# Attention with a gated unit on one core: store buffers moved, three weight scalings on VectorE, and the exponential table loaded later

## The chip, the cores and the metric

The kernel runs on one core of one Trainium2 chip. The metric is the device time of the whole kernel in microseconds; a number of runs is given by its median. One more execution is taken with the hardware profiler, and all lines of profiles below come from such executions. PE is TensorE, PEld its weight loads, DVE is VectorE, ACT is ScalarE, POOL is GpSimd, SP is SyncE.

## The reference

Input `x` has 2048 rows of 640. It is normalised, and two things are computed from it: an attention over the last 512 keys and values of a cache with 32 heads of 192, and a gated unit with 1536 inner columns. All inputs are bfloat16.

```
W = min(4096, max(256, Sk // 4))                  # 512 of 2048 keys
q = (x @ wq).reshape(B, Sq, 32, 192)              # wq: 640 x 6144
k, v = k_cache[:, :, Sk-W:, :], v_cache[:, :, Sk-W:, :]
p = softmax(q k^T * 192 ** -0.5)
s = (p v).reshape(B, Sq, 6144) @ wo               # wo: 6144 x 640

h = sigmoid(x @ w_gate) * (x @ w_up)
g = silu(h @ w_down)
out = x0 + s * g          # x = layernorm(x0) in the formulas above
```

## The kernel before

**Two phases.** The first phase (to about 165 us) normalises `x`, transposes it, and computes the gated unit in four stages of 512 rows (`s` from 0 to 3). A stage ends with four parts `q`; each part multiplies by `w_down` (L495), takes a sigmoid on ACT (L502), a product on VectorE into a buffer `gB_sb` of `gpool` (L503), and stores it to DRAM from POOL's queue (L519). The second phase is the attention. It goes through 16 runs `r`, one for each pair of a group of four heads (`g`, 8 groups) and a half of the rows (`pi`).

**Order.** Every engine has its own instruction stream in the order in which the code emits it; nothing is reordered between engines, and waits are by semaphores. The pools of the two phases use the same memory: when the pools under `bctx` are closed, those of the second phase (`acc_pool` first, then `wo_pool`, `qT_pool`, `e_pool` for the exponentials, and so on) are laid from the same place, and an instruction that first writes a tile waits for the last users of what lay there before.

**Query projection by sums.** The queries are not one plain product with `wq`. Each weight chunk `c` (five of them, 128 of the 640 rows) comes as a tile `raw` (L202, from POOL's queue; three buffers), is multiplied by a power of two and turned to float16 in place (`scale_raw`, L216), and is then copied and combined into four weight tiles (`copy_w`, `sum_w`: L225 and L234 to L238 where POOL does it). `second_w(c)` (L240) does that for the second group on POOL, and then issues the load of the chunk three further on. The second group's weight tiles lie in the accumulator tile `acc_hi`, which is not needed until later. `query_slots` (L568) gives eleven slots of ten matmuls (L560). After a slot, partial sums go from PSUM to a ring of four buffers `qp` (L579 on ACT in the first run, L581 on VectorE in others), and sums of PSUM and such a partial make `qT` (L594, VectorE).

**Around the change.** In the last stage of the first phase the second group's chunks 0, 1 and 2 are scaled on ACT after parts 1, 2 and 3 (L510). Then the weights of the output projection are loaded (`load_wo(0)`, SP's queue), ACT computes one exponential of a dummy value so that its table of exponentials is loaded (L744), and the eleven slots of the first run follow; after the first three of them stand `second_w(0)`, `(1)` and `(2)`. Then run 0 begins: 16 score steps `k` (`stage_s`, L638: six matmuls L646 into one of two pairs of banks, then an exponential L650 on ACT), between which the slots for the next run's queries lie (`q_after`). After steps 7 and 11 of run 0 chunks 3 and 4 are scaled on ACT, each followed by its `second_w`. Then eight value stages (`stage_pv`, L652: 16 matmuls L660, a reciprocal L666 and a product L667 on VectorE into `o_st`); after each second one `o_st`, which has two buffers, is transposed by SP's queue (L673). The output projection (L703) of a run lies in the value part of the next one.

`scale_k` (L142) multiplies a key tile of the same shape as `raw` on VectorE.

Of the kernel before, what the change touches and what calls it, by code (L numbers as in the profile page):

```python
# [8 lines left out]
AF = mybir.ActivationFunctionType  # L9
ALU = mybir.AluOpType  # L10
BF16 = mybir.dt.bfloat16
F32 = mybir.dt.float32
F16 = mybir.dt.float16
# [4 lines left out]
def kernel(  # L18
# [13 lines left out]
    nc = tc.nc  # L32
# [46 lines left out]
    def bank2():  # L79
        if bank_order:  # L80
            b = bank_order.pop(0)
        else:
            b = ring.pop(0)
            ring.append(b)
        return ps_all[:, 2 * b:2 * b + 2, :]

    def flat(ps):
        return ps.rearrange("p b n -> p (b n)")
# [26 lines left out]
    mx, w_up, w_down = (w_sc[:, i:i + 1] for i in range(3))  # L115
# [61 lines left out]
    def scan_fold(wm, i):  # L177

        v = scan_t[i]
        bits = (wm[:] if i == 0 else v).bitcast(I32)  # L180
        nc.vector.tensor_single_scalar(bits, v.bitcast(I32), 0x7FFF7FFF, op=ALU.bitwise_and)
        if i > 0:
            nc.vector.tensor_tensor(wm[:], wm[:], v, ALU.max)
# [15 lines left out]
    def load_raw(g, c, eng):  # L199
        raw = raw_pool.tile([P, 2, GC], BF16, name="raw")  # L200
        for r in (LO, HI):
            eng.dma_start(raw[r], wq_r[:, c, :, g * GC:(g + 1) * GC])  # L202
        raw_t[g, c] = raw
# [9 lines left out]
    def sums_w(g, c, r, i):  # L213
        return w_t[g][i][r, c].rearrange("p (j h e) -> p h j e", h=2, e=HF)

    def scale_raw(g, c):  # L216
        raw = raw_t[g, c][:]
        nc.scalar.activation(raw.bitcast(F16), raw, AF.Copy, scale=w_up)  # L218

    def copy_act(dst, src):  # L220
        nc.scalar.activation(dst, src, AF.Copy)  # L221
# [1 line left out]
    def copy_w(g, c, copy):  # L223
        for k, r in enumerate((LO, HI)):
            copy(sums_w(g, c, r, 0), part_w(g, c, r, k, 0))  # L225

    def scale_w(g, c):
        scale_raw(g, c)
        copy_w(g, c, copy_act)

    def sum_w(g, c, tt=nc.vector.tensor_tensor, copy=copy_act):
        a = slice(0, P)
        TA, TB, TC = (sums_w(g, c, a, i) for i in range(1, 4))
        tt(TB, part_w(g, c, a, 1, 1), part_w(g, c, a, 0, 1), ALU.subtract)  # L234
        tt(TA, TB, part_w(g, c, a, 0, 0), ALU.add)
        copy(sums_w(g, c, HI, 2), part_w(g, c, HI, 1, 1))
        tt(TC, part_w(g, c, a, 1, 0), TA, ALU.subtract)
        tt(sums_w(g, c, HI, 1), part_w(g, c, HI, 0, 1), part_w(g, c, HI, 0, 0), ALU.subtract)  # L238

    def second_w(c):  # L240

        copy_w(1, c, nc.gpsimd.tensor_copy)
        sum_w(1, c, nc.gpsimd.tensor_tensor, nc.gpsimd.tensor_copy)
        load_raw(1 + (c + 3) // NCD, (c + 3) % NCD, nc.gpsimd)


    with ExitStack() as bctx:
        gpool = bctx.enter_context(tc.tile_pool(name="gpool", bufs=4))
        wB = bctx.enter_context(tc.tile_pool(name="wB", bufs=1))
        bwork = bctx.enter_context(tc.tile_pool(name="bwork", bufs=2))  # L250
        bone = bctx.enter_context(tc.tile_pool(name="bone", bufs=1))
        hpool = bctx.enter_context(tc.tile_pool(name="hpool", bufs=2))
        xpool = bctx.enter_context(tc.tile_pool(name="xpool", bufs=3))
        xin_pool = bctx.enter_context(tc.tile_pool(name="xin_pool", bufs=1))
        xt_pool = bctx.enter_context(tc.tile_pool(name="xt_pool", bufs=1))
# [177 lines left out]
        for s in range(NST):  # L433
# [57 lines left out]
            for q in range(TQ):  # L491
                oB_ps = flat(bank2())
                for f in range(NF):
                    for d0, dsz in d_chunks:
                        nc.tensor.matmul(  # L495
                            oB_ps[:, d0:d0 + dsz], lhsT=hT_sb[:, f, q * P:(q + 1) * P],
                            rhs=wd_sb[:, f, d0:d0 + dsz],
                            start=(f == 0), stop=(f == NF - 1),
                        )
                gB_sb = gpool.tile([P, D], BF16, name="gB_sb")  # L500
                sg = bone.tile([P, D], F32, name="sg")
                nc.scalar.activation(sg[:], oB_ps[:, 0:D], AF.Sigmoid)  # L502
                nc.vector.tensor_tensor(gB_sb[:], oB_ps[:, 0:D], sg[:], ALU.mult)  # L503
                if (s, q) in folds_q:
                    scan_fold(wmax, folds_q[s, q])
                if s == 3:
                    if q == 0:
                        scale_w(0, NCD - 1)
                    else:
                        scale_raw(1, q - 1)  # L510
                    if q == 1:
                        sum_w(0, NCD - 1)
                        load_raw(1, 2, nc.gpsimd)
                    if q < 3:
                        sum_x(pi, 3 + q, sw)
                    else:
                        load_k((1, 0))
                t = s * TQ + q
                nc.gpsimd.dma_start(gB_d[t * P:(t + 1) * P, :], gB_sb[:])  # L519
# [27 lines left out]
    def load_wo(g):  # L547
        pool = late["wo"] if g == NG - 1 else wo_pool
        eng = nc.scalar if 0 < g < NG - 1 else nc.sync
        wo_g = pool.tile([P, G * PC, D], BF16, name="wo_g")  # L550
        eng.dma_start(wo_g[:], wo_r[:, g * G * PC:(g + 1) * G * PC, :])
        wo_t[g] = wo_g
# [188 lines left out]
    last = len(runs) - 1  # L741
    qT_t, E_t, oT_t, ost_t = {}, {}, {}, {}
    load_wo(0)
    nc.scalar.activation(mx, w_up, AF.Exp, scale=0.0)  # L744
    slots = query_slots(0, True, (2, 3), (4, 5), (0, 1, 6))
    for n, k in enumerate((0, 1, 7, 2, 3, 8, 4, 5, 9, 6, 10)):
        slots[k]()
        if n < 3:
            second_w(n)
    sum_at = {0: (0,), 1: (1,), 3: (2,), 4: (3,), 6: (4,)}  # L750
    scale_at = {0: (2,), 3: (3,), 4: (4,)}
    q_after = {1: (0,), 2: (1,), 3: (2,), 4: (3,), 5: (4,), 6: (5, 6), 8: (7,), 10: (8,), 12: (9,), 14: (10,)}
# [1 line left out]
    for r, (pi, g) in enumerate(runs):  # L754
        s_list = [(i, pp, c) for i in range(2) for pp in range(G) for c in range(KC)]
        q_list = query_slots(r + 1, False, (0, 1), (2, 3), (2, 3, 1)) if r < last else []
        wo_list = [(r - 1, i, q) for i in range(2) for q in range(TQ)] if r > 0 else []
        for k, x in enumerate(s_list):
            stage_s(r, *x, k)
            for j in q_after.get(k, ()) if q_list else ():  # L760
                q_list[j]()
            if r == 0 and k in (7, 11):
                scale_raw(1, 3 + k // 8)
                second_w(3 + k // 8)
            if r == last and k % 2 == 1:
                ring[:] = [k // 2 % 2]
                stage_wo(*wo_list[k // 2])
        if r == last:
            wo_list = []
            bank_order[:] = [2, 3, 0, 1] * 2  # L770
        else:
            bank_order[:] = [0, 1, 0, 1] + [2, 3, 0, 1] * 3 if r > 0 else [2, 3, 0, 1] * 2
        ring[:] = [0, 1, 2, 3]

        new_t = g + 1 if pi == 0 and 0 < g < NG - 1 else None
        if new_t is not None:
            weight_tiles(new_t)
            scale_w(new_t, 0)
            scale_w(new_t, 1)
        elif pi == 1 and g + 1 < NG:  # L780
            scale_k((g + 1, 0))
            turn_k((g + 1, 0))
            load_k((g + 1, 1))
        if r == last - 1:
            qctx.close()
            for name, n in (("wo", 1), ("gate", 4 * TQ), ("fin", 2 * TQ), ("fout", 4), ("ost", 4), ("tmp", 2)):
                late[name] = ctx.enter_context(tc.tile_pool(name=f"late_{name}", bufs=n, **rs))
            load_wo(g)
            prepare(r)

        pv_list = [(i, pp, h) for i in range(2) for pp in range(G) for h in range(2)]
        done = 0
        for k, x in enumerate(pv_list):
            stage_pv(r, *x)
            if k == 3 and pi == 1 and g + 1 < NG:
                scale_k((g + 1, 1))
                turn_k((g + 1, 1))
                if g + 2 < NG:
                    load_k((g + 2, 0))
            share = (k + 1) * len(wo_list) // len(pv_list)  # L800
            while done < share:
                stage_wo(*wo_list[done])
                done += 1
            if new_t is not None:
                for c in sum_at.get(k, ()):
                    sum_w(new_t, c)
                    if c + 3 < NCD:
                        load_raw(new_t, c + 3, nc.gpsimd)
                for c in scale_at.get(k, ()):
                    scale_w(new_t, c)  # L810
        if new_t is not None and g + 2 < NG:
            for c in range(3):
                load_raw(g + 2, c, nc.gpsimd)
        if pi == 1 and g + 1 < NG:
            for pp in range(G):
                load_v(g + 1, pp, nc.scalar)
        if pi == 0 and 0 < g < NG - 1:
            load_wo(g)
        if r == last - 1:
            prepare(last)  # L820
# [32 lines left out]
```

The softmax here doesn't subtract the row's maximum and nothing guards it: scores larger than these inputs give would overflow.

## Time and profile before

| | |
|---|---|
| three timed runs, median | 914.24 us (913.92 to 914.3) |
| the profiled execution's own time | 915.81 us |
| its span in the trace | 914.0 us |
| granted clock of PE, mean over the span | 0.997 |
| PE busy | 894.2 us, 98% |
| VectorE busy | 650.2 us, 71% |
| ScalarE busy | 438.0 us, 48% |
| GpSimd busy | 178.6 us, 20% |
| DMA | 100.38 MB, mean 110 GB/s |

The profiled execution lasts 1.8 us longer than its span, which goes from the first to the last instruction in the trace. A line of a timeline gives start, duration, engine, line of the code, operation, output and inputs, how many were merged, and in brackets the idle time before it and what ended it. A line of the stretches gives, for each engine in the order PE, PEld, DVE, ACT, POOL, its busy time and how many instructions, then the clock granted to PE, the busy share of the DMA engines and GB/s.

### The profile page before, as it was taken

The page shows a single profiled execution, that of the slowest core. Times are in us where ns is not written, and L with a number is a line of the kernel's source. Part 1 is how long each engine was busy: PE and PEld are TensorE (multiplying, and loading weights), DVE is VectorE, ACT ScalarE, POOL GpSimd, SP SyncE. Part 2 cuts the span into 40 slices and gives each one's busy share as a digit, 9 for nine tenths or more (in the row PEclk, how much of TensorE's full clock was granted, in tenths as well). Part 3 has the DMA queues.
Part 4 walks back from the last instruction along what each step waited for, and adds up shares of the span by engine and source line. Part 5 has one row for each costly group of instructions (what it writes and reads, how often), then busy time and mean ns, then how long its engine had stood idle before and what let it go on. Part 6 is the DMA issues. An engine that isn't in the chain of part 4 may idle for free. (4 is left out here: it accounts for less than half of the span.)

```text
span 914.0 us, 18466 instructions
## 1 busy us (share of the span) xinstructions
PE 894.2 (98%) x7712; PEld 531.7 (58%) x7791; DVE 650.2 (71%) x1087; ACT 438.0 (48%) x513; POOL 178.6 (20%) x220
## 2 busy tenths in 40 slices
PE   8999999889999999999999999999999999999997
PEld 5545454446665656565656565656565656565665
DVE  4879956556667866786678667866786678666566
ACT  4323346673428542854285428542854285424240
POOL 0051112582000200020002000200020000001972
PEclk9999999999999999999999999999999999999999
DMA  9993374415271828193718271827192805264745
GB/s 287 259 267 91 93 153 94 117 53 89 41 133 10 190 45 131 20 172 53 131 19 182 41 134 18 182 45 130 18 180 43 134 17 132 42 116 138 158 112 122
DMA packets 186757, 100.38 MB, mean 110 GB/s; under 512 B 153584, under 2 KB 179056, under 8 KB 186672
## 3 DMA queue, kind: packets, MB, share of 16 engines
q1 hardware_dynamic: 157776, 57.85, 32.0%
q0 software_dynamic: 9408, 29.93, 14.3%
q10 hardware_dynamic: 19488, 11.41, 5.2%
q8 instruction: 61, 1.00, 0.5%
q14 instruction: 24, 0.20, 0.1%
HBM read 57.87 MB, written 5.24 MB: 69 GB/s over the span
## 5 line engine op out<-in xcount | busy, mean ns | idle before, releaser
L650 ACT ACTIVATE E<-ps_all 128x1024 bf16<-128x1024 f32 x256 | 253.4, 1022 | 308.2 <-PE ps_all L646 260.9
L703 PE MATMUL ps_all<-wo_g,oT 128*128 128x128 bf16 (+2 forms) x1480 | 225.2, 295 | 3.3
L646 PE MATMUL ps_all<-qT,kT 64*128 64x512 bf16 x1536 | 195.4, 376 | 4.1 <-ACT E L650 2.2
L660 PE MATMUL ps_all<-v_sb,E 128*128 128x193 bf16 x2048 | 189.5, 247 | 0.0
L660 PEld LDWEIGHTS <-E 128*128 128x128 bf16 x2048 | 168.6, 98 | 18.0 <-issue 6.4
L703 PEld LDWEIGHTS <-oT 128*128 128x128 bf16 x1542 | 121.4, 98 | 79.6 <-issue 3.6
L594 DVE TENSOR_TENSOR qT<-ps_all,qp 128x512 bf16<-128x512 f32 x176 | 116.8, 688 | 55.0 <-PE ps_all L560 45.0
L581 DVE COPY qp<-ps_all 128x512 f32<-128x512 f32 x150 | 100.8, 689 | 61.4 <-PE ps_all L560 61.4
L646 PEld LDWEIGHTS <-kT 64*128 64x128 bf16 x1536 | 75.8, 94 | 93.4 <-issue 10.7
L667 DVE TENSOR_TENSOR o_st<-ps_all,rden 128x768 bf16<-128x768 f32 x128 | 122.5, 957 | 9.6 <-DMA oT<-o_st 5.2
L202 POOL DMA_DIRECT2D raw<-in_A_wq_dram x80 | 48.0, 605 | 275.5 <-ACT wB L221 238.1
L135 POOL DMA_DIRECT2D k_sb<-in_A_k_cache_dram x32 | 32.7, 1027 | 277.1 <-DVE o_st L667 121.3
L218 ACT ACTIVATE raw<-raw,w_sc 128x1536 f16<-128x1536 bf16 x40 | 63.0, 1574 | 2.0 <-DMA raw<-in_A_wq_dram 1.1
L560 PE MATMUL ps_all<-XA,wA 64*128 64x512 f16 x420 | 54.0, 386 | 2.1 <-ACT qp L579 1.7
L560 PE MATMUL ps_all<-XB,wB 64*128 64x512 f16 x420 | 52.6, 376 | 0.4 <-ACT qp L579 0.4
L495 PE MATMUL ps_all<-wd_sb,hT_sb 128*128 128x128 bf16 (+1 forms) x377 | 52.4, 298 | 0.4
L560 PE MATMUL ps_all<-X,w 64*128 64x512 bf16 x420 | 51.9, 376 | 0.1
L738 DVE TENSOR_TENSOR acc<-ps_all,acc 128x640 f32<-128x640 f32 x48 | 39.5, 823 | 15.3 <-PE ps_all L703 14.9
L451 DVE TENSOR_TENSOR hT_sb<-ps_all,sig_sb 128x512 bf16<-128x512 f32 x48 | 32.4, 682 | 22.5 <-ACT sig_sb L450 11.8
L450 ACT ACTIVATE sig_sb<-ps_all 128x512 bf16<-128x512 f32 x48 | 28.0, 596 | 40.1 <-PE ps_all L445 37.1
L666 DVE RECIPROCAL rden<-ps_all 128x4 f32<-128x4 f32 x128 | 23.1, 181 | 33.0 <-PE ps_all L660 31.9
L738 DVE TENSOR_TENSOR acc_hi<-ps_all,acc_hi 128x640 f32<-128x640 f32 x48 | 39.3, 819 | 7.7 <-PE ps_all L703 7.7
(114 smaller groups left out, 744.3 us busy)
## 6 DMA issues: line engine op xcount, KB each, us to landing
raw<-in_A_wq_dram POOLq DMA_DIRECT2D x80, 192.0 KB, 3.8
k_sb<-in_A_k_cache_dram POOLq DMA_DIRECT2D x32, 192.0 KB, 6.0
wo_g<-in_A_wo_dram ACTq DMA_DIRECT2D x6, 960.0 KB, 6.9
v_sb<-in_A_v_cache_dram ACTq DMA_DIRECT2D x28, 192.0 KB, 3.9
gB_d<-gB_sb POOLq DMA_DIRECT2D x16, 160.0 KB, 3.7
gBa_sb<-gB_d SPq DMA_DIRECT2D x16, 160.0 KB, 4.1
xa_sb<-in_A_x_dram SPq DMA_DIRECT2D x16, 160.0 KB, 4.1
out_dram<-o_sb SPq DMA_DIRECT2D x15, 160.0 KB, 1.8
```

Of the source, the lines that this page charges most:

```text
L202: eng.dma_start(raw[r], wq_r[:, c, :, g * GC:(g + 1) * GC])
L218: nc.scalar.activation(raw.bitcast(F16), raw, AF.Copy, scale=w_up)
L495: nc.tensor.matmul(oB_ps[:, d0:d0 + dsz], lhsT=hT_sb[:, f, q * P:(q + 1) * P], rhs=wd_sb[:, f, d0:d0 + dsz], start=(f == 0), stop=(f == NF ...
L560: nc.tensor.matmul(ps_all[:, b, :], lhsT=w(r, c), rhs=x[r, c, :], start=(first and k == 0), stop=(k == len(cs) - 1), skip_group_check=True,)
L581: nc.vector.tensor_copy(dst, part(b))
L594: nc.vector.tensor_tensor(q_out(i, u, pp), part(b), t[:], ALU.add)
L646: nc.tensor.matmul(ps[:, b, :], lhsT=kT[h, c * PC + j, :], rhs=qT_t[r][i, j][h, pp, :], start=(j == 0), stop=(j == PC - 1),)
L650: nc.scalar.activation(E_t[r, i, pp][:, c, :, :], ps, AF.Exp, scale=scale_qk)
L660: nc.tensor.matmul(o_ps[:, q // 2, q % 2, 0:DH + 1], lhsT=E[:, c, h, q * P:(q + 1) * P], rhs=vt[:, c, 0:DH + 1], start=(c == 0), stop=(c = ...
L667: nc.vector.tensor_tensor(o_st[:, :, h * DH:(h + 1) * DH].rearrange("p (b i) d -> p b i d", b=2), o_ps[:, :, :, 0:DH], rden[:].to_broadcas ...
L703: nc.tensor.matmul(oA[:, d0 - base:d0 - base + dsz], lhsT=oT_t[r, i, pp][:, q * PC + j, :], rhs=wo_t[runs[r][1]][:, cc, d0:d0 + dsz], star ...
L738: nc.vector.tensor_tensor(acc[t][:], oA[:, 0:D], acc[t][:], ALU.add)
```

## The change

- The pool `gpool` of the gate's store buffers is opened after `hpool` instead of first. All of the first phase's pools that stood behind it move down, and its own place is now where the second phase has the tiles of exponentials `E`. The accumulators lie over weight tiles of the gated unit instead of over store buffers too.
- `scale_raw` can run on VectorE (a multiplication by the same scalar). Chunk 2 of the second group is scaled there after the seventh slot of the first run (n = 6, before its `second_w(2)`) instead of on ACT ahead of the slots, and `second_w(2)` itself moves from n = 2 to n = 6. Chunks 3 and 4 are scaled on VectorE after score steps 3 and 7 of run 0 instead of on ACT after steps 7 and 11, each again followed by its `second_w`.
- The dummy exponential with its table load comes after the third slot (n = 2) instead of ahead of the first.

The instructions of PE, POOL and SP are the same ones in the same order on each of these engines.

```diff
-    def scale_raw(g, c):
+    def scale_raw(g, c, on_act=True):
         raw = raw_t[g, c][:]
-        nc.scalar.activation(raw.bitcast(F16), raw, AF.Copy, scale=w_up)
+        if on_act:
+            nc.scalar.activation(raw.bitcast(F16), raw, AF.Copy, scale=w_up)
+        else:
+            nc.vector.tensor_scalar(raw.bitcast(F16), raw, w_up, None, op0=ALU.mult)
...
-        gpool = bctx.enter_context(tc.tile_pool(name="gpool", bufs=4))
         wB = bctx.enter_context(tc.tile_pool(name="wB", bufs=1))
         bwork = bctx.enter_context(tc.tile_pool(name="bwork", bufs=2))
         bone = bctx.enter_context(tc.tile_pool(name="bone", bufs=1))
         hpool = bctx.enter_context(tc.tile_pool(name="hpool", bufs=2))
+        gpool = bctx.enter_context(tc.tile_pool(name="gpool", bufs=4))
...
                 if s == 3:
                     if q == 0:
                         scale_w(0, NCD - 1)
-                    else:
+                    elif q < 3:
                         scale_raw(1, q - 1)
...
-    nc.scalar.activation(mx, w_up, AF.Exp, scale=0.0)
     slots = query_slots(0, True, (2, 3), (4, 5), (0, 1, 6))
     for n, k in enumerate((0, 1, 7, 2, 3, 8, 4, 5, 9, 6, 10)):
         slots[k]()
-        if n < 3:
-            second_w(n)
+        if n == 2:
+            nc.scalar.activation(mx, w_up, AF.Exp, scale=0.0)
+        elif n == 6:
+            scale_raw(1, 2, on_act=False)
+        if n in (0, 1, 6):
+            second_w(min(n, 2))
...
-            if r == 0 and k in (7, 11):
-                scale_raw(1, 3 + k // 8)
-                second_w(3 + k // 8)
+            if r == 0 and k in (3, 7):
+                scale_raw(1, 3 + k // 4, on_act=False)
+                second_w(3 + k // 4)
```

## The prediction

> **What bounds the kernel now.** I read the page first, then who waited for whom, then the timelines of the stretch that the diff touches (165 to 221 us: the query projection of the first run, its score stage, its value stage).
>
> ```profile
> PE 894.2 (98%) x7712; PEld 531.7 (58%) x7791; DVE 650.2 (71%) x1087; ACT 438.0 (48%) x513; POOL 178.6 (20%) x220
> ```
>
> ```profile
> PE ps_all L646 <- ACT E L650: 2.2, 2, 1.1
> PE ps_all L560 <- ACT qp L579: 2.1, 3, 1.7
> PE ps_all L646 <- DVE o_st L667: 1.8, 2, 1.6
> ```
>
> PE is busy for 894.2 of 914.0 us: the kernel is a line of matmuls, and only time in which PE stands or runs slowly can be won. The second view (who waited, how long in total, how often, longest) has PE's three largest waits, and all lie in this stretch. In PE's timeline:
>
> ```profile
> 164.83 3.41 PE L560 MATMUL ps_all<-X,w 64*128 64x512 bf16 x30
> 169.91 0.37 PE L560 MATMUL ps_all<-XA,wA 64*128 64x512 f16 x1 [1.67 <-ACT qp L579]
> 170.69 5.08 PE L560 MATMUL ps_all<-XA,wA 64*128 64x512 f16 x29 [0.41 <-DVE qT L594]
> ...
> 197.99 0.82 PE L646 MATMUL ps_all<-qT,kT 64*128 64x512 bf16 x6 [1.11 <-ACT E L650]
> ...
> 204.03 0.82 PE L646 MATMUL ps_all<-qT,kT 64*128 64x512 bf16 x6 [1.11 <-ACT E L650]
> ...
> 218.48 0.82 PE L646 MATMUL ps_all<-qT,kT 64*128 64x512 bf16 x6 [1.58 <-DVE o_st L667]
> ```
>
> The bracket is the idle time before the row and what ended it. Two more of 0.26 us follow the last. Note also that 30 matmuls took 3.41 us and then 29 took 5.08. The table by stretches (PE's clock is the third number from the end) says why:
>
> ```profile
> 168.30:170.70 2.40, 0.39 (x3) 0.10 (x3) 0.76 (x2) 2.39 (x5) 0.00 (x0) 1.00 1.14 294
> 171.30:174.70 3.40, 3.40 (x20) 1.49 (x18) 0.53 (x1) 1.73 (x4) 0.62 (x2) 0.52 0.30 72
> 216.90:220.70 3.80, 1.70 (x15) 0.70 (x16) 3.14 (x6) 1.30 (x2) 0.00 (x0) 1.00 0.31 68
> ```
>
> After the gap at 168.3 the clock was halved for 3.4 us; after the gap at 216.9 it was not. ACT's timeline shows who made the gaps:
>
> ```profile
> 166.28 1.57 ACT L218 ACTIVATE raw<-raw,w_sc 128x1536 f16<-128x1536 bf16 x1 [0.65 <-DMA raw<-in_A_wq_dram]
> 167.87 1.28 ACT L744 ACT_TABLE_LOAD   x1
> 169.16 0.20 ACT L744 ACTIVATE w_sc<-w_sc 128x1 f32<-128x1 f32 x1
> 169.28 1.55 ACT L579 ACTIVATE qp<-ps_all 128x512 f32<-128x512 f32 x3
> ...
> 195.46 1.57 ACT L218 ACTIVATE raw<-raw,w_sc 128x1536 f16<-128x1536 bf16 x1
> ```
>
> The first three query slots are done on PE at 168.24, but their copies out of PSUM stand behind a scaling and a table load. The two later scalings, this one and its twin at 201.50, sit between exponentials, each just ahead of a 1.11 us gap.
>
> [...]
>
> **The change part by part**, on the profiled execution's clock.
>
> *First scaling to VectorE, table load behind the third slot.* ACT ends its last sigmoid at 165.63 and is free. Copies (0.55 each) run as slots end: about 166.7, 167.75, 168.85. VectorE's adds (0.69) end at 167.4, 168.5, 169.55. Slot four needs the first copy and add, long done at 168.24: 1.67 + 0.41 = **2.08 us** gone. The table load then covers 168.85 to 170.3; ACT must make four copies by 172.5, when slots seven and later want them: 170.3 + 4 x 0.55 = 172.5, just in time. The stalls of 0.21 and 0.23 at 178 come from the four-buffer ring of partial sums, which is unchanged; they stay.
>
> *The half-rate stretch.* With no gap of 2 us it should not occur: 3.41 x 0.5 = **1.7 us** in the profiled execution. Whether the timed runs have it, the profile cannot say. The profiled execution took 915.81, the median 914.24: 1.57 apart, near 1.7. I take it that the timed runs lack it, and count 0 on the median.
>
> *Two scalings out of the score stage.* The exponentials (1.02 for a step in which PE takes at least 0.65, and 2.38 for two steps with a slot) keep up without them: 2 x 1.11 = **2.22 us** gone.
>
> *Three scalings on VectorE.* The nearest row is the key scaling L142, same shape on VectorE, bf16 to bf16: 616 ns. An f16 output I price alike; the upper bound is the 1.57 us that ACT takes. To this comes a wait for one POOL instruction, 0 to 0.91 us (L234's row), middle 0.45. The first stands between the adds of slots seven and eight (n = 6 and 7). Behind it, on VectorE's queue, are five adds; the last slot reuses the bank that the third of these frees. By my sums that add ends at 176.45 [...] and PE wants it at 176.6; with the middle wait 176.9: **+0.3 us**, from 0 to 1.1. The second, at score step 3, stands ahead of copies where VectorE has 0.44 us free a step: **+0.2 us**, from 0 to 0.4. The third, at step 7, meets free VectorE: 0.
>
> *The store buffers.* Both runs of second-group sums on POOL began late:
>
> ```profile
> 174.02 1.06 POOL L225 COPY acc_hi<-raw 64x384 f16<-64x384 f16 x2 [6.66 <-PE ps_all L560]
> ```
>
> The releaser named is not credible (an L560 matmul has no claim on that tile); 174.02 fits the last gate store, issued at 166.79 with a landing of up to 6.9 us. In the new stream that copy no longer waits for stores, so POOL starts about 167.4. Each chunk takes 7.1 us with its load: loads issue at 173.4, 180.5, 187.6, 194.7 and 202, the last 8 us earlier than now (210.1). No store's cost vanishes: the first exponential now waits for them. It comes at 178, they land by 174: 0. The `wo` load on SP now waits for old work on VectorE and goes up to 1.6 us later; its 7.6 us end nearly 70 us before its first use at 242.6: 0.
>
> *The gap at 216.9.* VectorE waited 4.35 us there for the first transpose of outputs, issued at 210.21, in the same moment as POOL's last weight load, and landing in 7.2 us; those in this stretch have a median of 4.7 and a minimum of 3.6. PE's wait of 1.58 + 0.26 + 0.26 = 2.1 us is what exceeds about 5 us. In the new run the transpose goes at about 204.6 and that load ends by 206: they touch only at the edge. I count **1.6 us** won; bounds 0 (still collides) and 2.1.
>
> Everything behind 221 us has PE at work with waits under 0.5 us, and its transfers follow compute rather than the clock, so the gain should reach the end. Sum: 2.08 + 2.22 + 1.6 - 0.3 - 0.2 = 5.4 us, plus 1.7 in the profiled execution: 915.81 - 7.1 = 908.7 for it; for the median 914.24 - 5.4 = **908.8**.
>
> **The rivals.**
> (a) *The timed runs do have the half-rate stretch*: 914.24 - 7.1 = 907.1. [...] Against: the 1.57 us. Chance 0.27.
> (b) *VectorE takes back part*: scalings of 1.57 us, [...] the transpose still late: 5.4 - 1.6 - 0.8 - 0.2 = 2.8, so 911.4. For it: VectorE is at 71% and in this stretch nearly full. Chance 0.17.
> (c) *Slower: VectorE's queue blocks at score step 3.* The scaling there waits for chunk 3's load; behind it are all query copies and adds, and PE waits for these two slots later. It begins at about 185.3. Load 3 issues at 173.4 and lands in 3.3 to 3.8: 8 us of cover. If POOL still started late (some other wait holds it to 174), it would land at 184, still in time. It decides from a landing at 186.5 on, and the kernel is slower if that is after 192; with 195, 917. Chance 0.05.
> (d) *The change moves nothing*: the copies wait for another thing at 168.3, so only gaps change name, 914. PSUM banks and both inputs are free there, which speaks against it. Chance 0.02.
>
> **How the numbers follow.** The forecast has 0.49. Of the cases, the forecast, (a) and (b) are faster by over 0.2% (1.8 us, about what a measurement of this kernel can tell from no change): 0.93. Same 0.02, slower 0.05. The range reaches from (a) with the transposes wholly cleared [...], 914.24 - 8.1 = 906.1, to just beyond (b), 911.6.
>
> **What would show it.** In the changed profile: PE has no row with 1.67 behind ACT's copies, the table load lies behind three L579 copies; clock 1.00 through 165 to 180; no 1.11 us gaps ahead of score matmuls; the first POOL copy at about 167.5; the scalings on VectorE near 0.62 us (a 1.0 or 1.6 breaks that term); VectorE's wait for the first transpose under 3 us. Wrong it is if a new PE gap of over 1 us follows a VectorE scaling, if the half-rate stretch comes back elsewhere, or if VectorE is seen to wait for a weight load.

## The result and the profile after

| | before | after |
|---|---|---|
| median | 914.22 us (913.92 to 914.3, 4 runs) | 906.97 us (906.74 to 907.29, 4 runs) |
| the profiled execution's own time | 915.81 us | 906.74 us |
| its span | 914.0 us | 905.0 us |

The ratio is 0.9922 with an interval of 0.9904 to 0.9939: 7.25 us faster. In a later set of runs the kernel after had 906.94 and the kernel before 915.25, ratio 0.9908 (0.9894 to 0.9923); why before varies is the first experiment's subject. The range held the result; the point, 908.8, was 1.8 us too slow, and rival (a), 907.1, comes closest. One execution of the kernel before, 946.37 us at a mean clock of 0.948, belongs to a slower state of the chip and is left out below.

Line numbers after are mostly three higher: L219 or L221 is the scaling on ACT or VectorE, L582 ACT's copy of a query sum, L649 a score matmul, L670 the product into `o_st`, L751 the table load.

PE's waits after (total, times, longest), without those of the start:

```profile
PE ps_all L563 <- ACT qp L582: 0.5, 2, 0.3
...
PE ps_all L563 <- DVE o_st L670: 0.3, 1, 0.3
PE ps_all L649 <- DVE o_st L670: 0.2, 1, 0.2
```

PE's timeline:

```profile
164.57 3.41 PE L563 MATMUL ps_all<-X,w 64*128 64x512 bf16 x30
167.82 3.40 PE L563 MATMUL ps_all<-XA,wA 64*128 64x512 f16 x30
171.06 2.41 PE L563 MATMUL ps_all<-XB,wB 64*128 64x512 f16 x20
173.78 0.37 PE L563 MATMUL ps_all<-XB,wB 64*128 64x512 f16 x1 [0.31 <-ACT qp L582]
174.38 1.24 PE L563 MATMUL ps_all<-XB,wB 64*128 64x512 f16 x9 [0.23 <-ACT qp L582]
...
176.96 1.48 PE L649 MATMUL ps_all<-qT,kT 64*128 64x512 bf16 x12
...
199.38 10.83 PE L663 MATMUL ps_all<-v_sb,E 128*128 128x193 bf16 x128
...
211.14 0.82 PE L649 MATMUL ps_all<-qT,kT 64*128 64x512 bf16 x6 [0.18 <-DVE o_st L670]
212.22 1.25 PE L563 MATMUL ps_all<-X,acc_hi 64*128 64x512 bf16 x10 [0.26 <-DVE o_st L670]
```

The gaps of 1.67 and 0.41 are gone, and the second thirty matmuls take as long as the first (3.40 beside 3.41; 5.08 for 29 before). The two gaps of 1.11 have no row here. Of the 2.1 us ahead of run 1's work 0.44 is left; the two waits of the ring of four, 0.31 and 0.23, stay. ACT:

```profile
168.02 0.60 ACT L582 ACTIVATE qp<-ps_all 128x512 f32<-128x512 f32 x1 [0.48 <-PE ps_all L563]
168.63 1.28 ACT L751 ACT_TABLE_LOAD   x1
169.93 0.20 ACT L751 ACTIVATE w_sc<-w_sc 128x1 f32<-128x1 f32 x1
170.04 2.04 ACT L582 ACTIVATE qp<-ps_all 128x512 f32<-128x512 f32 x4
```

VectorE's scalings and its wait for the first transpose:

```profile
173.61 0.61 DVE L221 TENSOR_SCALAR raw<-raw,w_sc 128x1536 f16<-128x1536 bf16 x1
...
184.47 0.61 DVE L221 TENSOR_SCALAR raw<-raw,w_sc 128x1536 f16<-128x1536 bf16 x1
...
191.44 0.98 DVE L221 TENSOR_SCALAR raw<-raw,w_sc 128x1536 f16<-128x1536 bf16 x1
...
209.05 0.96 DVE L670 TENSOR_TENSOR o_st<-ps_all,rden 128x768 bf16<-128x768 f32 x1 [2.63 <-DMA oT<-o_st]
```

And the table by stretches over the place where PE's clock had been halved (third number from the end):

```profile
164.60:168.30 3.70, 3.70 (x37) 1.69 (x38) 2.70 (x4) 2.18 (x4) 3.51 (x6) 1.00 0.80 185
168.30:170.70 2.40, 2.40 (x26) 1.10 (x24) 0.69 (x1) 2.37 (x5) 2.26 (x3) 1.00 0.94 326
170.70:176.90 6.20, 5.66 (x51) 3.24 (x49) 4.39 (x8) 3.47 (x7) 5.47 (x9) 1.00 0.44 136
```

**Where the time came from.** I take the start of the same matmul in the two profiled executions. The first query matmul begins at 164.83 and 164.57; the first score matmul at 181.32 and 176.96; the first value matmul at 206.06 and 199.38; the first one of run 1's queries with `acc_hi` weights at 220.64 and 212.22. So the query slots gave 4.36 - 0.26 = 4.10 us, the score stage 2.32, the value stage 1.74: 8.16 us together. The spans differ by 9.0; the other 0.8 lies ahead of the first query matmul (0.26) and behind 221 us.

### The profile page after: what moved, and what is told of

The parts are those of the page before. It is cut to its first block, busy times and chain, and to the rows that moved or that the text cites. A ratio compares the mean times of both kernels' runs of the same rounds, so it can differ in the third digit from the quotient of the medians.

```text
span 905.0 us, 18469 instructions
## 1 busy us (share of the span) xinstructions
PE 891.8 (99%) x7712; PEld 531.5 (59%) x7791; DVE 651.7 (72%) x1090; ACT 433.3 (48%) x510; POOL 178.8 (20%) x220
## 4 chain that ended last, share of the span: by engine, by line
PE 97%; DVE 1%; issue 1%; ACT 1%; DMA 0%; SPq 0%; DVEq 0%
PE ps_all L706 23%; PE ps_all L563 20%; PE ps_all L663 19%; PE ps_all L649 18%; PE ps_all L448 11%; PE ps_all L498 6%; PE ps_all L362 1%; DMA x_sb<-in_A_x_dram 0%; ACT E L653 0%; ACT qp L582 0%; DVE qT L597 0%; DVE ps_all L720 0%; DVE o_st L670 0%; DVE stats L326 0%; DVE tmp L717 0%
## 5 line engine op out<-in xcount | busy, mean ns | idle before, releaser
L649 PE MATMUL ps_all<-qT,kT 64*128 64x512 bf16 x1536 | 194.8, 376 | 0.2 <-DVE o_st L670 0.2
L670 DVE TENSOR_TENSOR o_st<-ps_all,rden 128x768 bf16<-128x768 f32 x128 | 122.5, 957 | 7.8 <-DMA oT<-o_st 3.4
L649 PEld LDWEIGHTS <-kT 64*128 64x128 bf16 x1536 | 75.7, 94 | 89.1 <-issue 6.2
L219 ACT ACTIVATE raw<-raw,w_sc 128x1536 f16<-128x1536 bf16 x37 | 58.3, 1575 | 1.3 <-DMA raw<-in_A_wq_dram 0.4
L563 PE MATMUL ps_all<-XA,wA 64*128 64x512 f16 x420 | 51.9, 376 | 0.0
```

What stands on the lines that cost most here:

```text
L563: nc.tensor.matmul(ps_all[:, b, :], lhsT=w(r, c), rhs=x[r, c, :], start=(first and k == 0), stop=(k == len(cs) - 1), skip_group_check=True,)
L649: nc.tensor.matmul(ps[:, b, :], lhsT=kT[h, c * PC + j, :], rhs=qT_t[r][i, j][h, pp, :], start=(j == 0), stop=(j == PC - 1),)
L670: nc.vector.tensor_tensor(o_st[:, :, h * DH:(h + 1) * DH].rearrange("p (b i) d -> p b i d", b=2), o_ps[:, :, :, 0:DH], rden[:].to_broadcas ...
```

## The experiments

**E1: before again, for its clock.** No edit.

> The kernel before once more, unchanged, for the granted clock of every timed execution. Theory (the timed runs lack the half-rate stretch of 3.41 us that the profiled execution of before has): most timed executions show a mean clock of 0.999 to 1.000 and times near 914.2, and an execution that has the stretch (mean clock 0.997) takes about 1.7 us longer. Rival (a) of the prediction (all of them have it): every execution shows 0.997 and none differs by 1.7 us.

Its own 13 runs had a median of 915.12. With all other runs of before from this and the later sets there are 59, median 915.43. In 30 of them the mean clock of PE was 0.997 or less, median 916.07; in 29 it was 0.998 or more, median 914.46. The mean clock is not a clean sign, however, since it counts the end of the span too, where PE has no more work. In the kernel after:

```profile
900.00:905.00 5.00, 0.00 (x0) 0.00 (x0) 1.30 (x5) 0.00 (x0) 0.83 (x1) 0.72 0.33 102
```

The reduced clock there falls on no matmul, but it gives this execution a mean of 0.998 without any stretch at half rate before. The stretch alone, 3.41 us at half rate in 914, makes 0.998 as well (before has 0.50 in every 0.1 us from 171.5 to 174.8, and 0.70 and 0.74 in the 0.1 us on either side). Of the traces of all runs, the four with the stretch (before, E1, E3, E4) have 0.997 and the ten without it 0.998 to 1.0. So I read 0.997 or less as having it (30 executions), 0.999 or more as not having it (14, median 914.0), and leave the 15 at 0.998 open: half to three quarters of the executions have it. What it costs is best read from the traces: the same 29 matmuls take 5.08 us with it and 3.40 without it (E7), 1.7 us more. Neither my "none" nor the rival's "all" holds. The four runs of the first comparison, all near 914.2, look like the kind without; their clocks are not on record.

**E2: the first part alone.** The kernel before, with

```diff
-                    else:
+                    elif q < 3:
                         scale_raw(1, q - 1)
...
-    nc.scalar.activation(mx, w_up, AF.Exp, scale=0.0)
...
-        if n < 3:
-            second_w(n)
+        if n == 2:
+            nc.scalar.activation(mx, w_up, AF.Exp, scale=0.0)
+        elif n == 6:
+            scale_raw(1, 2, on_act=False)
+        if n in (0, 1, 6):
+            second_w(min(n, 2))
```

> The kernel before with the first part alone: chunk 2 scaled on VectorE after the seventh slot, table load after the third; store buffers and chunks 3 and 4 as before. Theory: PE's gaps of 1.67 and 0.41 us go and nothing is lost to the scaling, 2.1 us faster on the median (912.1), 3.8 us if the half-rate stretch was in the timed runs. The two gaps of 1.11 us and the one ahead of the value stage's end stay, the latter perhaps longer, since POOL's last load does not move while PE comes 2 us sooner. Rival (VectorE takes part of it back): 1.0 to 1.8 us.

911.26 us beside 915.14, ratio 0.9964 (0.995 to 0.9978). Against the trace of E1 the query slots come out 3.99 us shorter (1.7 of it the clock), and, which I had not expected of this part, the value stage 1.08 us:

```profile
211.22 0.96 DVE L670 TENSOR_TENSOR o_st<-ps_all,rden 128x768 bf16<-128x768 f32 x1 [2.25 <-DMA oT<-o_st]
...
214.41 0.96 DVE L670 TENSOR_TENSOR o_st<-ps_all,rden 128x768 bf16<-128x768 f32 x1 [1.06 <-DMA oT<-o_st]
```

The first transpose, issued at 206.06 and so 2.4 us ahead of POOL's last load (208.42), now lands in 5.2 us; instead the second one is late, and PE waits 1.27 us ahead of run 1's queries. One of the five executions took 913.85 us at a clock of 0.997, although the trace of another has no gap left at 168 us; where that execution ran slowly is not known.

**E3: chunks 3 and 4 alone.** The kernel before, with

```diff
             if r == 0 and k in (7, 11):
-                scale_raw(1, 3 + k // 8)
+                scale_raw(1, 3 + k // 8, on_act=False)
```

> The kernel before with chunks 3 and 4 scaled on VectorE, after steps 7 and 11 as before; all else as before. Theory: the two gaps of 1.11 us ahead of score matmuls go, 2.2 us faster (912.0). VectorE has room there, so nothing comes back. Rival: the scaling waits for a POOL instruction and holds the copies behind it, 1.5 us or less. The gap at the end of the value stage may change either way, since POOL's last load moves with the scaling.

911.69 us, ratio 0.9966 (0.9954 to 0.9979): 3.4 us. The score stage gave 2.41, the value stage again 1.11, since PE comes sooner there and POOL's last load does not (209.40, transposes from 207.49).

**E4: the store buffers alone.** `gpool` opened behind `hpool` in the kernel before, nothing else.

> The kernel before with the store buffers moved alone. Theory: POOL's first copy starts at about 167.4 instead of 174.0, but chunk 3 is still scaled on ACT at 195.5, so POOL waits there and its last load still goes at about 209 to 210, in the moment of the first output transpose: no gain, 914.2 (within 0.3). Rival (the late POOL work itself holds something up): 0.5 to 2.1 us faster with the gap of 1.58 us smaller.

914.61 us, ratio 0.9995 (0.9986 to 1.0005): no difference that these runs can tell. POOL:

```profile
167.23 1.08 POOL L225 COPY acc_hi<-raw 64x384 f16<-64x384 f16 x2
...
197.01 1.05 POOL L225 COPY acc_hi<-raw 64x384 f16<-64x384 f16 x2 [8.44 <-ACT raw L218]
```

It starts 6.8 us sooner and gives it all back at chunk 3, where it waits for ACT; its last load goes at 210.00, the first transpose at 210.12, and the gap in front of run 1 even grew (2.19 beside 1.58).

**E5: the change without the store buffers.** The kernel after with `gpool` first.

> The kernel after, but with the store buffers where they were. Theory: POOL's first copy falls back to about 173.7, so its loads issue at 179.6, 186.8, 194, 201.2 and 208.4 and the last two lie among the output transposes at 203.5 to 212. The first transposes land late again and PE's wait at the end of the value stage grows from 0.44 us to 1.2 or 2.1: 0.8 to 1.7 us slower than the kernel after, 907.8 to 908.7. VectorE's scaling at score step 3 (184.5) finds its chunk landed (183.5), with 1 us to spare. Rival (the buffers do not matter): 907.0. Rival (c) of the prediction in small: the scaling waits for its chunk and PE for VectorE, a new gap of over 1 us at 186 to 190.

906.59 us (906.24 to 907.25), ratio 0.9903 (0.9891 to 0.9915): the same as the whole change, and my expectation of 0.8 to 1.7 us more was wrong.

```profile
201.47 1.20 POOL L202 DMA_DIRECT2D raw<-in_A_wq_dram  x2 [0.30 <-POOL acc_hi L241]
...
208.62 1.20 POOL L202 DMA_DIRECT2D raw<-in_A_wq_dram  x2 [0.30 <-POOL acc_hi L241]
```

The first transpose, issued at 203.54, lies between these two loads and lands in 5.1 us; VectorE waits 2.23. What counts is that no load starts with the first transpose, and PE's coming 6.7 us sooner does that with or without the buffers' move. The value stage is even 0.38 us shorter here than in the kernel after (12.46 beside 12.84). One scaling met more of POOL's work than any in the kernel after:

```profile
184.57 1.36 DVE L221 TENSOR_SCALAR raw<-raw,w_sc 128x1536 f16<-128x1536 bf16 x1
```

PE has no gap behind it: between the slots and the end of the score stage it waits nowhere.

**E6: the table load alone.** The kernel before; the dummy exponential behind the third slot (n == 2), all scalings on ACT as they were.

> The kernel before with only the table load moved behind the third slot; chunk 2 is still scaled on ACT ahead of the first copies. Theory: the first copy can start when that scaling ends (167.85), 1.4 us sooner than before; PE's gap of 1.67 shrinks to about 0.2 and the wait for VectorE's add stays at 0.4 to 0.7; with a gap of under 1 us the half-rate stretch is gone. 1.2 us of gap, 0.8 us for the stretch on the average (it was in 18 of 39 timed executions of before, which took 1.8 us more), and up to 0.8 at the end of the value stage, where the transposes come sooner than the last load: 912.3 to 913.2 beside a before of 915.1. Rival (the scaling alone makes the gap): 914.5 or more.

911.5 us, ratio 0.9956 (0.9944 to 0.9968): as much as E2, and more than I had expected, as the value stage is 1.39 us shorter than in E1 and not 0.8 at most. PE's gap of 1.67 is down to 0.33, the 0.41 stays, and the clock was 0.999 or 1.0 in all five runs.

**E7: the collision by itself.** The kernel before, with

```diff
-    def second_w(c):
+    def second_w(c, load=True):
...
-        load_raw(1 + (c + 3) // NCD, (c + 3) % NCD, nc.gpsimd)
+        if load:
+            load_raw(1 + (c + 3) // NCD, (c + 3) % NCD, nc.gpsimd)
...
-                second_w(3 + k // 8)
+                second_w(3 + k // 8, k == 7)
...
             load_k((g + 1, 1))
+            if r == 1:
+                load_raw(2, 2, nc.gpsimd)
```

> The kernel before with only its fifth weight load of POOL's chain (chunk 2 of the third group, issued at 210.1 as the first output transpose starts) issued after the key load of run 1 instead. Theory (the transpose lands late because that load moves in the same moments): the first transpose lands in about 5 us instead of 7.2, VectorE's wait of 4.35 us falls to 2.3 or less, PE's 2.1 us at 216.9 fall to 0 to 0.5: 1.6 to 2.1 us faster than before. Rival (the first transposes are slow of themselves, four in 11 us): 7.2 us and 2.1 us remain, no change.

913.44 us beside 915.8, ratio 0.9973 (0.9962 to 0.9983), a little more than the 1.6 to 2.1 us expected. The first transpose, issued at 208.25, lands in 4.8 us instead of 7.2:

```profile
213.10 0.96 DVE L668 TENSOR_TENSOR o_st<-ps_all,rden 128x768 bf16<-128x768 f32 x1 [1.93 <-DMA oT<-o_st]
```

and PE has no gap of more than 0.3 us there. One load that starts with the transposes cost before more than 2 us: the value stage takes 12.17 us instead of the 14.59 of E1. The same trace shows more on the clock. PE's timeline, then the stretches:

```profile
169.63 0.37 PE L561 MATMUL ps_all<-XA,wA 64*128 64x512 f16 x1 [1.66 <-ACT qp L580]
170.42 3.40 PE L561 MATMUL ps_all<-XA,wA 64*128 64x512 f16 x29 [0.41 <-DVE qT L595]
```

```profile
168.10:170.50 2.40, 0.46 (x3) 0.17 (x4) 0.83 (x2) 2.39 (x5) 0.00 (x0) 1.00 1.14 285
170.50:174.00 3.50, 3.50 (x34) 1.83 (x35) 1.06 (x2) 2.22 (x5) 0.50 (x2) 1.00 0.44 95
```

It is the same gap, 1.66 + 0.41, and this time no half rate follows. The eight executions fall into two groups, 911.45 to 912.37 and 913.31 to 913.86 us, and each group has two with a clock of 0.998, which shows again that this figure decides nothing. Without the stretch the query slots take 14.80 us, 2.41 more than in the kernel after: the stop cost more than its idle 2.07. Part of that is the one matmul between the two gaps, which holds PE for 0.37 us where 30 in a row take 3.41.

**E8: each VectorE scaling twice.** The kernel after, with

```diff
             nc.vector.tensor_scalar(raw.bitcast(F16), raw, w_up, None, op0=ALU.mult)
+            nc.vector.tensor_scalar(raw.bitcast(F16), raw.bitcast(F16), 1.0, None, op0=ALU.mult)
```

> The kernel after with each of the three VectorE scalings followed by a second multiplication of the same tile in place by 1.0 (another 0.6 us on VectorE, at each place). Theory now (VectorE's queue has room behind each of them, as the profile after shows no PE gap behind a scaling): 0 to 0.4 us slower than the kernel after. Rival (b) and the prediction's terms of 0.3 and 0.2 us for one scaling (the room is used up): 0.8 to 1.6 us slower, with new PE gaps behind VectorE's adds.

907.72 us (907.54 to 908.14), 0.75 us above the kernel after: between the two. The score stage is 1.01 us longer than in the kernel after, 0.84 of it at one place, the last scaling, behind score step 7:

```profile
194.19 1.26 PE L564 MATMUL ps_all<-XA,wA 64*128 64x512 f16 x10 [0.84 <-DVE qp L585]
```

At the other two places the second multiplication takes 0.56 and 0.74 us of VectorE; the slots grow by 0.15 us and the rest of the score stage by 0.17. The value stage, which PE reaches later, gives 0.50 back.

**E9: after again.** No edit, beside the next three.

> The kernel after once more, unchanged, on the chip of the next three, and for its granted clock. Theory: 906.6 to 907.3, with no execution that has a half-rate stretch (clock 0.998 or more in all).

906.94 us (906.64 to 907.57), clock 0.999 or 1.0 in every run.

**E10: the table load first, the scalings on VectorE.** The kernel after with the dummy exponential back ahead of the first slot.

> The kernel after with the table load back ahead of the first slot; the three scalings stay on VectorE. Theory: ACT is free at 165.4, loads the table until 166.9 and ends the first copy at 167.5 and VectorE the first add at 168.2, where PE wants them at 167.8: a gap of 0 to 0.5 us and nothing else, since a table load alone (1.5 us with its exponential) fits into the 3.2 us that the first three slots take. 907.0 to 907.5. Rival (the table load is what made the gap, and its place is what counts): PE's gap of 1.2 us or more comes back, at times with the half-rate stretch, 908.2 or more.

906.95 us (906.56 to 907.52): no difference.

```profile
165.21 1.28 ACT L747 ACT_TABLE_LOAD   x1
166.50 0.20 ACT L747 ACTIVATE w_sc<-w_sc 128x1 f32<-128x1 f32 x1
166.61 1.81 ACT L582 ACTIVATE qp<-ps_all 128x512 f32<-128x512 f32 x3
```

The copies end in time. With E6: each of the two edits removes most of the gap, and the kernel with both is not told from the kernel with either.

**E11 and E12: what is left.** The kernel after, with the eight low accumulators as one tile, in which run 0 puts its third and fourth output tile (E11), and also the first run's partial sums, in seven places (E12, which alone has the lines from `if on_act` to `return t`):

```diff
-    acc = [acc_pool.tile([P, D], F32, name=f"acc{t}") for t in range(2 * TQ)]
+    acc_lo = acc_pool.tile([P, 2 * TQ, D], F32, name="acc_lo")
+    acc = [acc_lo[:, t, :] for t in range(2 * TQ)]
+    lo_flat, lo_n = acc_lo.rearrange("p t d -> p (t d)"), [0]
...
+            if on_act:
+                n0 = 512 * (lo_n[0] % 7)
+                lo_n[0] += 1
+                t = lo_flat[:, n0:n0 + 512]
+                copy(t, b, act)
+                return t
...
+            if r == 0 and i == 1:
+                o0 = 3584 + 768 * pp
+                ost_t[0] = lo_flat[:, o0:o0 + 768].bitcast(BF16).rearrange("p (q d) -> p q d", q=TQ)
+            else:
```

> The kernel after with the third and fourth output tile of run 0 laid into accumulators that are not yet in use, so that no product waits for the first transposes. Theory: VectorE's wait of 2.63 us and PE's 0.18 + 0.26 us at 211 to 212 go: 0.3 to 0.5 us faster than the kernel after. Rival (another wait takes their place, such as PSUM banks): no difference.

> As the run before, and the partial sums of the first run's query slots also laid into accumulators not yet in use, seven places instead of the ring of four. Theory: ACT's copies of the third query no longer wait for VectorE's adds, PE's 0.31 + 0.23 us at 174 go as well: 0.8 to 1.0 us faster than the kernel after, 906.0. Rival (VectorE's queue, with a scaling in the middle, is the next to be late): 0.3 to 0.5 us.

906.24 us (905.71 to 907.09) and 906.21 us (906.0 to 906.49) beside 906.94 of E9: 0.7 us faster by the medians, E11 more than expected and E12 no better than E11. The ranges of E11 and E9 overlap, but the trace of E11 has a value stage of 12.06 us beside 12.85 in E9. In it the 0.18 and 0.26 us are gone. In E12 the two waits for ACT's copies give way to one for VectorE, as the rival said:

```profile
176.30 0.80 PE L565 MATMUL ps_all<-XC,wC 64*128 64x512 bf16 x5 [0.44 <-DVE qT L605]
```

The slots are 0.44 us shorter than in E9, but the score stage is 0.36 longer, with a wait of 0.20 for a copy on VectorE behind the last scaling, which took 1.28 us there. E11 and E12 have the lowest medians of all, below both kernels; between each other they aren't told apart.

## Why the prediction was right, and by how much it missed

- *What bounds it.* Right: all the gain that the traces locate came from PE's gaps and slow stretch between 165 and 221 us, and behind that the shift stayed: between run 1's first queries and the end the same instructions of E1 and E9 keep their distance within 0.12 us.
- *The first scaling and the table load.* Right for the gaps of 1.67 and 0.41, with the table load between the copies where I had put it. That both edits were needed was my assumption; E6 and E10 show that one suffices nearly. The size was too low: I took the idle time, 2.08 us, for the worth of the stop, and E7 puts it at 2.41.
- *The half-rate stretch.* Wrong as a statement on timed runs. I read 1.57 us between one profiled execution and a median of three as a sign that they lack it, and counted 0. By the clocks it is in half to three quarters of 59 executions, at 1.7 us each: 0.9 to 1.3 us on a mean. For the four runs of the comparison, three of which I had seen, the 0 fits their times, so this term isn't what the point missed by. E7 has the same gap followed by full rate, clock 1.00 from 170.5 to 174.0. I hadn't allowed for the same gap being followed by it in some executions and not in others. Some 2.1 us of idle time with a matmul in the middle were followed by it in four traces of five; what decides between them isn't shown.
- *The costs on VectorE.* Too high: +0.3 and +0.2 us came out as nothing that shows. The scalings took 0.61 us at two places and 0.98 at the third, and 1.36 in E5: within the row of L142 (0.62 us) and the bound for a wait (0.91 us). That VectorE would wait for a POOL instruction was an assumption when I priced it; the last section has the rows it can be read from. That the scalings cost PE nothing is read from the gaps; no run leaves them out. The place was wrong, too: I had called the third, at step 7, free. E8 and E12 show that it has the least room.
- *The score stage.* 2.22 predicted, 2.32 measured.
- *The gap at the value stage.* 1.6 predicted, 1.74 measured, and the collision is shown by E7. But the step that I gave as the reason, POOL's loads coming 8 us sooner by the buffers' move, isn't needed: without it (E5) the first transpose falls between two loads. I credited an edit that brings nothing here, and that the number came out right was luck of the timetable. Alone the buffers bring nothing (E4), as POOL then waits for ACT.
- *POOL's start.* Right: 167.09 for a forecast of about 167.4. That the wait was for the last gate store is shown by E4, where moving their buffers alone ends it. The traces name different releasers for the same wait: that store in E3 and E7, the load of the output weights in E1, a matmul in before.
- *Rivals.* (a) is true of half to three quarters of the executions, though by their times not of the four compared. (b) did not come about. (c) did not either: chunk 3's scaling began at 184.47 with its load issued at 173.00. (d) fell.

The sum for a median without the stretch was 5.4, and 7.25 was measured. Of the 1.8 us missing, 0.5 are the costs that did not come. Another 0.6 lie in the three stops, which were worth more than I priced them at: 2.41 for 2.08, 2.32 for 2.22 and 1.74 for 1.6. The rest, 0.8, is what the traces of before and after have ahead of the first query matmul and behind run 1's first queries. Over all fourteen traces that matmul begins between 164.38 and 165.05 us, and what follows run 1's first queries lasts 692.7 to 693.7 us, with no order by kernel; so it looks like the spread of executions, but that isn't shown.

## What to carry to other kernels

Before crediting an edit, look at what else in the same change moves the same wait: here two edits each sufficed for one gap, and a third only shifted work that then waited elsewhere. A load that started together with a transpose went with 2.1 us of waits on PE; issued 2.4 us later (E2) it went with 1.27, as the next transpose was late, and 2.1 us earlier (E5) with 0.23. So a faster part ahead of such a meeting can change the sum by more than its own gain, or less. And one profiled execution is no sample of a state that comes and goes: run the old kernel ten times with its clock before pricing it, and look in a trace where in the span the clock is low: a mean also counts time in which PE has no work.

## What the runs showed of the hardware

- The gap of about 2 us in PE's work at 168 us was followed by 3.4 us at half rate in four of the five traces that have it (before, E1, E3, E4, not E7), and by the mean clocks in half to three quarters of 59 executions of one kernel; it cost 1.7 us when it was. The 2.1 us of gaps from 216.9 on in before were followed by none (clock 1.00 from 216.9 to 228). With the gap cut to 0.74 us or less (E6, E9, E10) no execution had a clock under 0.999; one of the five of E2, whose trace has no gap there, had 0.997.
- VectorE's scaling and POOL's copies and sums take longer where they meet. In the kernel after, the third scaling took 0.98 us instead of 0.61, and POOL's copy (L239), 0.50 us elsewhere, took more just where a scaling ran:

```profile
184.60 0.84 POOL L239 COPY acc_hi<-raw 64x384 f16<-64x384 f16 x1
...
192.06 0.72 POOL L239 COPY acc_hi<-raw 64x384 f16<-64x384 f16 x1
```

The excess is 0.37 us for VectorE (0.75 in E5, where the POOL sum beside it takes 0.91) and 0.34 and 0.22 for POOL. The longer scalings end 0.42 us behind the end of the POOL instruction that was running beside them: at 192.42 behind 192.00 in after, 199.63 behind 199.21 in E3, 185.93 behind 185.51 in E5, 192.76 behind 192.34 in E8. That looks like VectorE waiting for that instruction to end.
- One load of two halves of 192 KB, issued within 0.15 us of the first transpose, delayed it from 4.8 us (E7, without that load) to 7.2 or 7.8 us (before, E4); with a load issued 1.3 us ahead of it or 2.4 us behind it, the transpose landed in 5.4 (after) or 5.2 us (E2).
